# 16-token inverse blocks for chunks 0 to 3, with a new order of the first transfers, weights and merges

## The chip, the core and the metric

The kernel runs on one core of one Trainium2 chip. The metric is the device time of one execution in microseconds; the kernel before has a median of 960.33 over 14 runs (955.47 to 970.36).

## What is computed

Two blocks, one after the other. The first is a recurrence over 768 tokens for each of 4 x 8 heads of 40 channels; the second is an MLP over the 3072 tokens.

```python
for t in range(S):
    y[:, :, t] = np.einsum('bhd,bhde->bhe', rt, state)
    Sa = np.einsum('bhde,bhe->bhd', state, at)
    state_decay = state * wt[:, :, None, :] - np.einsum('bhd,bhe->bhde', Sa, bt)
    state = state_decay + np.einsum('bhd,bhe->bhde', vt, kt)
...
h = x @ w_in                      # 3072 x 320 by 320 x 2048
g = h * (1.0 / (1.0 + np.exp(-h)))
return g @ w_out                  # 2048 x 320
```

## The kernel before

**Tiling.** The recurrence is computed in 12 chunks of 64 tokens. A chunk has two units (m = 0, 1), each with two batches (`be`) and their eight heads. Within a chunk the sequential part is a triangular system of 64 tokens for each head, and its solution is a multiplication with the inverse of a unit triangular matrix. Across chunks the state is carried (`Gbd`).

**A chunk's steps.** `pre` has two steps: `scale` (a running product of the decay by scans L238, its reciprocal on VectorE L240, products on POOL L241 and L243, and two squares with sums on ACT for a range check) and `scores` (products of a and b, L216, masked by L224 into `sbs`, and eight small DMAs of the diagonal 32 x 32 blocks to a DRAM buffer `md`, L259). `chain` has keys (transposes, L392), right (L216, L402, L414), solve (L436, L454), read (L490 and the mask L498), write (L512, L522, then the state update L535, L539 and the output `yx` L544, sent to DRAM as `xs`, L550), and turn (transposes of the state, L474).

**The inverse.** Every two chunks share one inverse. The 128 partitions of `mi` hold the 128 diagonal blocks of 32 x 32 (two chunks, 16 heads, two batches, two halves of 32 tokens). `row(t)` does one row of back substitution on VectorE, one multiply (L281) and one sum (L287), for t = 30 down to 0. `back` writes the result to DRAM as it is (`zd`) and turned (`xd`, after copies by ACT and VectorE). `merge` then has three steps for each chunk: `fetch` reads zd and xd back into `XT`, tokens on partitions (L311, L314); `first` and `second` complete the 64 x 64 inverse from its 32 x 32 halves by two products on TensorE (L326, L343) with copies on ACT (L336, L353).

**Weights.** The MLP's weights arrive as 64-bit words in 40 pieces and are turned into 32-bit ones by five VectorE and three ACT instructions each (`weights`, L147 to L164). `load_weights` issues a piece's load on SP's queue five pieces ahead (three ahead in the second half), into rooms in the buffer of the MLP's `gts` (first half), and in `room`, `mi` and `tmp`.

**The MLP.** `moe(c)` takes two chunks (512 tokens): `fetch` reads `xs`; eight blocks of L577 and L582 with sigmoid (L585) and product (L586); products with w_out (L593); then the second half of the hidden channels the same way.

**Order.** The framework keeps each engine's instructions in order, in an order that follows the program and its own estimate; `weave` interleaves lists of steps. At the start, the four units of chunks 0 and 1 are loaded and prepared, then the first inverse runs with eight pieces of weights among its rows, then the merges of both chunks and chunk 0's steps with twelve pieces, then chunk 1 with fourteen pieces and chunk 2's `pre`, then the first MLP's first twelve steps with chunk 3's `pre`, the last six pieces and the second inverse. After that each chunk's steps are woven with eight steps of the MLP before it.

A matmul of 32-bit operands appears as two records in the profile.

Of the kernel before, what the change touches and what calls it, by code (L numbers as in the profile page):

```python
# [9 lines left out]
F32 = mybir.dt.float32  # L10
# [31 lines left out]
def kernel(  # L42
# [15 lines left out]
    nc = tc.nc  # L58
# [39 lines left out]
    XI = sb.tile([128, 32, 32], F32, name="XI")  # L98
# [13 lines left out]
    nc.vector.memset(XI, 0.0)  # L112
    nc.vector.memset(XI.rearrange("p s t -> p (s t)")[:, 0 : 32 * 32 : 33], 1.0)

# [16 lines left out]
    NW = len(pieces)  # L131
    rooms = {}

    def load_weights(n):

        if n == 0:
            rooms["gts"] = sb.tile([128, 4, 4 * WS], I32, name="room4", tag="gts")
        if n < NW // 2 and n % 5 < 4:
            rooms[n] = rooms["gts"][:, n % 5]
        else:  # L140
            tag = "room" if n < NW // 2 else ("room", "mi", "tmp")[n % 3]
            rooms[n] = sb.tile([128, 4 * WS], I32, name="room", tag=tag)
        for lo, hi, src in pieces[n][1]:
            raw = rooms[n][lo:hi, 0 : 2 * WS]
            nc.sync.dma_start(raw.rearrange("p (i x) -> p i x", x=256) if len(src.shape) == 3 else raw, src)

    def weights(n):  # L147
        dst, room = pieces[n][0], rooms[n]
        words = room[:, 0 : 2 * WS].rearrange("p (c two) -> p c two", two=2)
        lo, hi = words[:, :, 0], words[:, :, 1]  # L150
        e, f = room[:, 2 * WS : 3 * WS], room[:, 3 * WS : 4 * WS]
        shr, band, bor = ALU.logical_shift_right, ALU.bitwise_and, ALU.bitwise_or
        nc.vector.tensor_scalar(out=e, in0=hi, scalar1=20, scalar2=0x7FF, op0=shr, op1=band)
        nc.vector.tensor_scalar(out=f, in0=hi, scalar1=0xFFFFF, scalar2=None, op0=band)
        nc.scalar.activation(out=e, in_=e, func=AF.Relu, scale=2.0**23, bias=low)  # L155
        nc.scalar.activation(out=f.bitcast(F32), in_=f, func=AF.Copy, scale=2.0**-20, bias=1.0)
        nc.scalar.activation(out=lo.bitcast(F32), in_=lo.bitcast(U32), func=AF.Copy, scale=2.0**-52)
        nc.vector.scalar_tensor_tensor(out=e, in0=hi, scalar=-(1 << 31), in1=e, op0=band, op1=bor)
        f, lo, e = (x.bitcast(F32) for x in (f, lo, e))
        nc.vector.tensor_tensor(out=f, in0=f, in1=lo, op=ALU.add)  # L160
        nc.vector.tensor_tensor(out=dst, in0=f, in1=e, op=ALU.mult)
        ahead = 5 if n + 5 < NW // 2 else 3
        if n + ahead < NW and (n + 5 < NW // 2 or n + ahead >= NW // 2):
            load_weights(n + ahead)  # L164
# [105 lines left out]
    def inverse(md):  # L270
        steps = []
        xd = dr.tile([128, 32, 32], F32, name="xd", bufs=2)
        zd = dr.tile([128, 32, 32], F32, name="zd", bufs=2)
        mi = sb.tile([128, 32, 32], F32, name="mi")
        tmp = sb.tile([128, 32, 32], F32, name="tmp")
        for h in range(2):
            nc.sync.dma_start(mi[64 * h : 64 * h + 64], md[64 * h : 64 * h + 64])

        def row(t):
            n = 31 - t  # L280
            nc.vector.tensor_tensor(  # L281
                out=tmp[:, 0:n, 0:n],
                in0=XI[:, t + 1 : 32, t + 1 : 32],
                in1=mi[:, t, t + 1 : 32].unsqueeze(1).to_broadcast([128, n, n]),
                op=ALU.mult,
            )
            last = nc.vector.tensor_reduce(out=XI[:, t + 1 : 32, t], in_=tmp[:, 0:n, 0:n], axis=AX.X, op=ALU.add)  # L287
            mark["row"] = last.ins

        for t in reversed(range(31)):  # L290
            steps.append(partial(row, t))

        def back():
            nc.sync.dma_start(zd, XI)
            turned = XI.rearrange("p t s -> p s t")
            nc.scalar.copy(out=mi[:, 0:16], in_=turned[:, 0:16])
            nc.vector.tensor_copy(out=mi[:, 16:32], in_=turned[:, 16:32])
            nc.sync.dma_start(xd, mi)

        steps.append(back)  # L300
        return steps, xd, zd

    def merge(n, xd, zd):
# [4 lines left out]
        def fetch():  # L308
            for be in range(2):
                at = 64 * (n % 2) + 32 * be  # L310
                nc.sync.dma_start(X[C * be : C * be + 32, :, 32:64], zd[at : at + 16].rearrange("q t s -> t q s"))  # L311
                for c in range(2):
                    r = C * be + 32 * c
                    nc.sync.dma_start(  # L314
                        X[r : r + 32, :, 32 * c : 32 * c + 32],
                        xd[at + 16 * c : at + 16 * c + 16].rearrange("q s t -> s q t"),
                    )

        def first():
            s = sbs[n].rearrange("p m j q t -> p (m j q) t")  # L320
            box["qq"] = sb.tile([128, N, 32], F32, name="qq", tag="tmp")
            pq = [bank("pq") for _ in range(2)]
            for h in range(N):
                for be in range(2):
                    r = C * be
                    nc.tensor.matmul(  # L326
                        pq[be][r + 32 : r + 64, h * 32 : h * 32 + 32],
                        lhsT=s[r : r + 32, h, 32:64],
                        rhs=X[r : r + 32, h, 32:64],
                        start=True,  # L330
                        stop=True,
                        tile_position=(r, r + 32),
                    )
            for be in range(2):
                R = slice(C * be + 32, C * be + 64)
                nc.scalar.copy(out=box["qq"][R].rearrange("p h t -> p (h t)"), in_=pq[be][R, 0 : N * 32])  # L336
# [291 lines left out]
    def invert(n):  # L628
# [3 lines left out]
        box = {}  # L632

        def begin():
            box["rows"], box["xd"], box["zd"] = inverse(md[0])

        def do(k, i):
            if i == 0:
                box[k] = merge(k, box["xd"], box["zd"])
            box[k][i]()  # L640
# [4 lines left out]
            + [lambda i=i: box["rows"][i]() for i in range(32)]  # L645
# [10 lines left out]
    for n in range(5):  # L656
        load_weights(n)
    convert = [partial(weights, n) for n in range(NW)]
    xs = dr.tile([DM, 4 * NM * C], F32, name="xs", bufs=2)
    for u in units[0]:  # L660
        load_rv(u)
# [3 lines left out]
    run(prepare(1))  # L665
    chains = {0: [chain(u, xs) for u in units[0]]}
    run([x[i] for i in range(2) for x in chains[0]])
    steps = invert(1)
    run(steps[0:1] + convert[0:8] + steps[1:32])
    queue = []  # L670
    with tc.issue_after(mark["row"]):
        for u in units[2]:
            load(u)
        run(steps[32:])
        steps = [x for pair in zip(*[x[2:] for x in chains[0]]) for x in pair]
        weave(late.pop(0) + steps, convert[8:20])
# [5 lines left out]
        weave(steps[0:4], convert[20:24])  # L682
        weave(steps[4:], convert[24:34], prepare(2))
    fetch, queue = moe(0, xs)
    fetch()
    with tc.issue_after(mark["turn"]):
        weave(queue[0:12], prepare(3) + convert[34:] + invert(3))
# [174 lines left out]
```

## Time and profile before

| | us |
|---|---|
| median of 14 runs | 960.33 |
| the profiled execution | 958.35 |
| its span | 956.6 |
| TensorE busy in the span | 806.9 (84%) |
| VectorE busy | 567.2 (59%) |
| ScalarE busy | 283.3 (30%) |
| POOL busy | 93.2 (10%) |
| mean granted TensorE clock | 0.918 |
| rows of all six inverses, L281 | 186 instructions, 99.1 |
| rows of all six inverses, L287 | 186 instructions, 93.1 |

The profile is of one execution. A row of a group gives the line, the engine, what is written from what, the count, the busy time and the mean duration of one. The chain of waits lists the pieces of work that ended last, each followed back to what released it. Slices are fortieths of the span.

### The profile page before, as it was taken

The page shows a single profiled execution, that of the slowest core. Times are in us where ns is not written, and L with a number is a line of the kernel's source. Part 1 is how long each engine was busy: PE and PEld are TensorE (multiplying, and loading weights), DVE is VectorE, ACT ScalarE, POOL GpSimd, SP SyncE. Part 2 cuts the span into 40 slices and gives each one's busy share as a digit, 9 for nine tenths or more (in the row PEclk, how much of TensorE's full clock was granted, in tenths as well). Part 3 has the DMA queues.
Part 4 walks back from the last instruction along what each step waited for, and adds up shares of the span by engine and source line. Part 5 has one row for each costly group of instructions (what it writes and reads, how often), then busy time and mean ns, then how long its engine had stood idle before and what let it go on. Part 6 is the DMA issues. An engine that isn't in the chain of part 4 may idle for free.

```text
span 956.6 us, 23746 instructions
## 1 busy us (share of the span) xinstructions
PE 806.9 (84%) x10210; PEld 551.0 (58%) x10210; DVE 567.2 (59%) x1113; ACT 283.3 (30%) x628; POOL 93.2 (10%) x90
## 2 busy tenths in 40 slices
PE   0301988589999659999989999989999899999996
PEld 0301877235587615787636866638875478755544
DVE  8699697989517697065992367970659714031111
ACT  2423564530243202342212352114322143210120
POOL 5300110320001101001010021100010000000000
PEclk9855786599999769999999999989999999999999
DMA  9773555620336531355513555323532313002001
GB/s 222 155 194 83 136 152 154 156 56 11 77 85 148 118 97 61 74 120 119 147 26 77 129 124 123 76 65 68 130 93 82 84 37 74 1 17 59 0 1 31
DMA packets 230831, 87.60 MB, mean 92 GB/s; under 512 B 194368, under 2 KB 221504, under 8 KB 230720
## 3 DMA queue, kind: packets, MB, share of 16 engines
q1 hardware_dynamic: 226496, 84.97, 36.7%
q10 hardware_dynamic: 4224, 1.05, 0.6%
q8 instruction: 82, 1.34, 0.6%
q14 instruction: 29, 0.24, 0.1%
HBM read 68.68 MB, written 17.30 MB: 90 GB/s over the span
## 4 chain that ended last, share of the span: by engine, by line
PE 55%; DVE 31%; DMA 4%; issue 3%; POOL 2%; SPq 2%; ACT 1%; POOLq 0%; DVEq 0%; ACTq 0%
PE po L593 14%; PE ph L577 10%; DVE tmp L281 8%; DVE XI L287 7%; PE pl L490 5%; PE ph L582 4%; DVE w L240 3%; PE pt L392 3%; PE pq L326 3%; PE po L343 3%; PE pm L216 2%; PE pgy L522 2%; PE pr L414 2%; PE pu L436 2%; DVE gts L586 2%
## 5 line engine op out<-in xcount | busy, mean ns | idle before, releaser
L577 PE MATMUL ph<-xt,wi_s 128*128 128x512 f32 x384 | 193.7, 640 | 33.6 <-DVE gts L586 16.2
L593 PE MATMUL po<-wo_s,gts 128*128 128x320 f32 x768 | 219.1, 438 | 2.2 <-DVE gts L586 2.1
L593 PEld LDWEIGHTS po<-wo_s,gts 128*128 128x128 f32 x768 | 141.8, 190 | 65.2 <-DVE gts L586 4.6
L577 PEld LDWEIGHTS ph<-xt,wi_s 128*128 128x128 f32 x384 | 70.9, 198 | 128.7 <-issue 66.3
L586 DVE TENSOR_TENSOR gts<-ph,sg 128x512 f32<-128x512 f32 x96 | 63.8, 682 | 102.0 <-ACT sg L585 102.0
L585 ACT ACTIVATE sg<-ph 128x512 f32<-128x512 f32 x96 | 52.9, 594 | 229.7 <-PE ph L582 229.6
L281 DVE TENSOR_TENSOR tmp<-XI,mi 128x1 f32<-128x1 f32 (+30 forms) x186 | 99.1, 533 | 11.8 <-DMA mi<-md 7.0
L287 DVE TENSOR_REDUCE XI<-tmp 128x1 f32<-128x1 f32 (+30 forms) x186 | 93.1, 500 | 4.6
L216 PE MATMUL pm<-a,kb 64*64 64x64 f32 x1536 | 48.9, 240 | 42.2 <-POOL kb L243 27.1
L243 POOL TENSOR_TENSOR kb<-kb,w 128x512 f32<-128x512 f32 x42 | 51.5, 1246 | 239.4 <-DVE w L240 175.2
L224 DVE TENSOR_TENSOR sk<-pm,ms 128x256 f32<-128x256 f32 x48 | 18.3, 420 | 92.0 <-PE pm L216 91.9
L216 PEld LDWEIGHTS pm<-a,kb 64*64 64x64 f32 x1536 | 39.6, 148 | 54.4 <-POOL kb L243 45.7
L240 DVE RECIPROCAL w<-W 128x512 f32<-128x512 f32 x21 | 70.3, 3346 | 0.7
L326 PE MATMUL pq<-XT,sb 32*32 32x32 f32 x768 | 26.4, 200 | 50.7 <-DMA XT<-zd 50.7
L241 POOL TENSOR_TENSOR a<-a,W 128x512 f32<-128x512 f32 x24 | 28.8, 1199 | 371.9 <-DMA a<-in_aT 209.6
L582 PE MATMUL ph<-xt,wl_s 64*128 64x512 f32 x192 | 60.9, 665 | 0.0
L498 DVE TENSOR_TENSOR vl<-pl,ml 128x512 f32<-128x512 f32 x48 | 31.0, 684 | 47.0 <-PE pl L490 47.0
L326 PEld LDWEIGHTS pq<-XT,sb 32*32 32x32 f32 x768 | 23.9, 115 | 57.1 <-ACT room L155 50.8
L490 PE MATMUL pl<-r,vut 64*128 64x64 f32 x768 | 49.8, 283 | 0.1
L490 PEld LDWEIGHTS pl<-r,vut 64*128 64x128 f32 x768 | 47.9, 196 | 2.6 <-issue 1.4
L483 ACT COPY GT<-pt 40x512 f32<-40x512 f32 x44 | 25.5, 580 | 73.9 <-PE pt L474 73.1
L522 PE MATMUL pgy<-vl,kt 128*64 128x104 f32 (+1 forms) x768 | 41.0, 259 | 0.1
(95 smaller groups left out, 924.3 us busy)
## 6 DMA issues: line engine op xcount, KB each, us to landing
a<-in_aT SPq DMA_DIRECT2D x24, 256.0 KB
kb<-in_bT SPq DMA_DIRECT2D x48, 128.0 KB
kb<-in_kT SPq DMA_DIRECT2D x48, 128.0 KB
vut<-in_vT SPq DMA_DIRECT2D x48, 128.0 KB
r<-in_rT SPq DMA_DIRECT2D x24, 256.0 KB
w<-in_wT SPq DMA_DIRECT2D x40, 128.0 KB
room<-in_w_out SPq DMA_DIRECT2D x20, 256.0 KB
room<-in_w_in SPq DMA_DIRECT2D x16, 256.0 KB
```

Source lines behind the costliest of these rows:

```text
L216: nc.tensor.matmul(pm[j][C * be : C * be + C, p * C : p * C + C], lhsT=u.kb[J, q, n, :], rhs=u.a[J, q, :], start=True, stop=True,)
L240: nc.vector.reciprocal(R, u.W[:, :, 1 : C + 1])
L281: nc.vector.tensor_tensor(out=tmp[:, 0:n, 0:n], in0=XI[:, t + 1 : 32, t + 1 : 32], in1=mi[:, t, t + 1 : 32].unsqueeze(1).to_broadcast([128 ...
L287: last = nc.vector.tensor_reduce(out=XI[:, t + 1 : 32, t], in_=tmp[:, 0:n, 0:n], axis=AX.X, op=ALU.add)
L326: nc.tensor.matmul(pq[be][r + 32 : r + 64, h * 32 : h * 32 + 32], lhsT=s[r : r + 32, h, 32:64], rhs=X[r : r + 32, h, 32:64], start=True, s ...
L490: nc.tensor.matmul(pl[j][:, q * C : q * C + C], lhsT=u.vut[J, q].rearrange("p n t -> p (n t)"), rhs=u.r[J, q, :], start=True, stop=True,)
L522: nc.tensor.matmul(pgy[be][J, p * N + last * D : p * N + N], lhsT=u.kt[:, P * be + p, J], rhs=u.vl[:, P * be + p, j, last * D :], start=u. ...
L577: in_order(nc.tensor.matmul(ph[n], lhsT=wi_s[:, k, at : at + 128], rhs=xt[:, k, :], start=k == 0, stop=False))
L582: in_order(nc.tensor.matmul(ph[n], lhsT=wl_s[R, i, :], rhs=xt[R, 2, :], start=False, stop=True))
L585: nc.scalar.activation(out=sg, in_=ph[n], func=AF.Sigmoid)
L586: nc.vector.tensor_tensor(out=box["gts"][:, (2 * i + n) % (NF // 2), :], in0=ph[n], in1=sg, op=ALU.mult)
L593: in_order(nc.tensor.matmul(po[:, 0:DM], lhsT=box["gts"][:, f, b * 128 : b * 128 + 128], rhs=wo_s[:, NF // 2 * half + f, :], start=f == 0, ...
```

## The change

The inverses of chunks 0 to 3 (`small(n)`) are done on blocks of 16 tokens: `inverse` takes N = 16, and each partition then holds two diagonal blocks that go through the rows together, so there are 15 rows instead of 31. A new step `sixteen`, called at the start of `first` for these chunks, completes the 32 x 32 inverses: 64 matmuls, a mask by VectorE (rows of a 32-group past its 16th), 96 matmuls, two additions by VectorE, two zeroings by POOL, four copies by ACT. `fetch` reads four more blocks of zd for these chunks. For chunks 0 and 1 the DMAs of xd go out on ACT's queue.

`load_rv` of chunk 0 moves from ahead of `prepare(0)` to after the issue of the read of `mi`; the first five pieces of weights are issued by ACT's queue; 24 pieces instead of 20 use the rooms in `gts`. A call of `weights` now does the first five instructions of piece n and the last three of piece n - 1. Six pieces instead of eight are placed ahead of the first inverse's rows, 13 in chunk 0, seven in chunk 1 and 15 calls in the first MLP. The merge of chunk 1 moves from ahead of chunk 0's solve to between its read and its write.

```diff
-        mi = sb.tile([128, 32, 32], F32, name="mi")
-        tmp = sb.tile([128, 32, 32], F32, name="tmp")
+        I = 32 // N
+        X, M = blocks(XIf), blocks(mif)
...
-            n = 31 - t
+            n = N - 1 - t
+            part = tmp[:, :, 0:n, 0:n]
             nc.vector.tensor_tensor(
-                out=tmp[:, 0:n, 0:n],
-                in0=XI[:, t + 1 : 32, t + 1 : 32],
-                in1=mi[:, t, t + 1 : 32].unsqueeze(1).to_broadcast([128, n, n]),
+                out=part,
+                in0=X[:, :, t + 1 : N, t + 1 : N],
+                in1=M[:, :, t, t + 1 : N].unsqueeze(2).to_broadcast([128, I, n, n]),
                 op=ALU.mult,
             )
...
+        def sixteen(s, pp):
+            pa = bank("pq")
+            for h in range(N):
+                for r in range(0, 128, 32):
+                    nc.tensor.matmul(
+                        pa[r : r + 32, h * 16 : h * 16 + 16],
+                        lhsT=s[r : r + 16, h, r % 64 : r % 64 + 32],
+                        rhs=X[r : r + 16, h, 32 - r % 64 : 48 - r % 64],
+                        start=True, stop=True, tile_position=(r, r),
+                    )
+            nc.vector.tensor_scalar(
+                out=pp, in0=pa[:, 0 : N * 16].rearrange("p (h t) -> p h t", h=N), scalar1=lower, scalar2=None, op0=ALU.mult
+            )
+            pe = bank("po")
+            for h in range(N):
+                for r in range(0, 128, 32):
+                    nc.tensor.matmul(pe[r : r + 16, h * 16 : h * 16 + 16], lhsT=pp[r : r + 32, h, :],
+                        rhs=X[r : r + 32, h, r % 64 + 16 : r % 64 + 32], start=True, stop=True, tile_position=(r, r))
+                for r in range(0, 128, 64):
+                    nc.tensor.matmul(pe[r : r + 32, 256 + h * 16 : 272 + h * 16], lhsT=X[r : r + 32, h, 0:32],
+                        rhs=pp[r : r + 32, h, :], start=True, stop=True, tile_position=(r, r))
...
+            for r in range(0, 128, 64):
+                nc.vector.tensor_tensor(
+                    out=X[r : r + 32, :, 32:48], in0=pe[r : r + 32, 1], in1=X[r : r + 32, :, 32:48], op=ALU.add
+                )
+                nc.gpsimd.memset(X[r + 32 : r + 64, :, 0:32], 0.0)
+            for r in range(0, 128, 32):
+                nc.scalar.copy(out=X[r : r + 16, :, r % 64 + 16 : r % 64 + 32], in_=pe[r : r + 16, 0])
...
     for n in range(5):
-        load_weights(n)
+        load_weights(n, nc.scalar)
...
-    for u in units[0]:
-        load_rv(u)
     run(prepare(0))
...
     run(prepare(1))
+    steps = invert(1)
+    run(steps[0:1])
+    for u in units[0]:
+        load_rv(u)
     chains = {0: [chain(u, xs) for u in units[0]]}
     run([x[i] for i in range(2) for x in chains[0]])
-    steps = invert(1)
-    run(steps[0:1] + convert[0:8] + steps[1:32])
+    run(convert[0:6] + steps[1:16])
...
-        weave(late.pop(0) + steps, convert[8:20])
+        steps[4:4] = late.pop(0)
+        weave(steps, convert[6:19])
...
-        weave(steps[0:4], convert[20:24])
-        weave(steps[4:], convert[24:34], prepare(2))
+        weave(steps[0:4], convert[19:21])
+        weave(steps[4:], convert[21:26], prepare(2))
...
-        weave(queue[0:12], prepare(3) + convert[34:] + invert(3))
+        weave(queue[0:12], prepare(3) + convert[26:] + invert(3))
```

## The prediction

> **What bounds the kernel now.** I read the forty slices first, for the stage that has room; then the chain of work that ended last, in order of time; then the busy times in the stretches between its landmarks.
>
> ```profile
> PE   0301988589999659999989999989999899999996
> ...
> DVE  8699697989517697065992367970659714031111
> ...
> PEclk9855786599999769999999999989999999999999
> ```
>
> A slice is 23.9 us. TensorE (PE) is nearly full from the eleventh slice (239 us) on; before that VectorE (DVE) is, and the TensorE clock is at half. So the change works in a stage bound by VectorE and a chain of dependent steps, and what it adds for chunks 2 and 3 falls where TensorE is full.
>
> ```profile
> 43.10 5.20 DMA mi<-md
> ...
> 84.45 1.17 DVE XI L287
> ...
> 91.34 3.71 PE pq L326 x64
> ...
> 106.07 1.54 PE pu L436 x26
> ...
> 171.39 1.20 DVE W L238 x2
> ```
>
> The first inverse's input lands at 48.3; its last row ends at 85.6; the merges of chunks 0 and 1 run from 91.34 to 106.07, then chunk 0's solve starts. At 171 VectorE still prepares chunk 3.
>
> ```profile
> 50.00:86.00 36.00, 0.00 (x0) 0.00 (x0) 34.24 (x70) 4.89 (x14) 0.00 (x0) 0.50 0.44 112
> 86.00:106.00 20.00, 13.41 (x256) 13.18 (x256) 15.39 (x38) 11.46 (x25) 3.65 (x3) 0.50 0.65 173
> ...
> 158.00:182.00 24.00, 9.62 (x128) 8.56 (x128) 22.84 (x56) 12.39 (x30) 3.88 (x3) 0.56 0.71 184
> 182.00:207.00 25.00, 22.39 (x80) 8.51 (x80) 22.18 (x40) 11.21 (x26) 5.98 (x5) 0.87 0.41 98
> ...
> 250.00:290.00 40.00, 39.76 (x784) 32.65 (x786) 8.55 (x18) 13.21 (x27) 2.36 (x2) 1.00 0.45 108
> ```
>
> Columns: stretch, length, busy us of PE, PE's weight loads, DVE, ACT, POOL, then granted clock, DMA share, GB/s. TensorE idles all through the first inverse (50 to 86) and more than half of 158 to 182; from 250 to 290 it has no gap. That is the trade: rows are taken from VectorE and small matmuls put on TensorE.
>
> **What the skill says.** (1) The Trainium skill, "VectorE: DVE Perf Modes", Specifications: 0.96 GHz. A row is one multiply and one reduce; the pair of 225 elements takes 0.85 us from start to start (59.55 to 60.40), that of 900 takes 2.26 (81.00 to 83.26): 2.09 ns an element, two passes at that clock, and 0.38 us fixed. Agrees. (2) "TensorEngine Tiling (Array Packing)", Instruction Overhead and Key Properties: a matmul has about 60 cycles of overhead, so narrow ones gain nothing, and a change of tiling mode drains the array. Agrees: at full clock 64 records of 32x32 took 1.34 us (276.98) and 32 of 64x64 0.69 (269.39), 21 ns each; 32 records between MLP matmuls took 1.12, 0.43 more. (3) "TensorE: Matmul & The Clock Gate", What's actually happening: half clock after idling, full after about 3.4 busy us. The drop agrees (0.50 from 50 to 86); the rise doesn't: 86 to 106 stays at 0.50 with TensorE 13.4 us busy. So I price the early merges cold. (4) "DMA: Bandwidth & Descriptors", Anatomy of one DMA: about 2 us fixed. The inverse's write was issued at 85.63 and its first read-back at 88.43, 2.8 later.
>
> **The change, stage by stage** (times of the profiled span; each matmul in the code is two records).
>
> *To the end of the first inverse: 85.6 becomes 55.5, 30.1 less.* Chunk 0's eight `md` DMAs no longer stand behind the 14 of load_rv and the first weights on SP's queue. Chunk 1's wait for its scores, ready at 32.5 as now: eight at 0.58 (16 took 9.28) and a `w` load put the read of `mi` at 38; now it is at 42.35 and lands after 5.2 more. I take 44. The weights' six issues move to ACT, 0.66 each, under waiting ACT time; the 14 loads come after `mi` and are wanted only by "right", then at 45. Converting pieces 0 to 5 stays under the wait for `mi` (VectorE idles 7.0 there now). Rows: 15 instead of 31, two blocks each: 15 x 0.38 + 2.09 ns x 2480 elements = 10.9 (31 x 0.38 + 2.09 ns x 10416 = 33.5 before), plus 0.75 for one score mask that sits among them. Merges don't hide this: TensorE idles.
>
> *From there to chunk 0's solve: 20.5 becomes 31, 10.5 more.* Read-back needs 7 us (four zd DMAs, 0.55 apart). The 128 records of sixteen()'s first product would be done at +11, but its VectorE mask stands in the queue behind two scans, a reciprocal (3.3), a copy and six converted pieces. The last five of these need ACT, which first issues xd, waits about 2.3 for it to land, and issues eight read-backs at 0.62: ACT is free at +10.5 and needs 5 more for five pieces. So the mask is at +16. Then 192 records, mask adds, 64 records, ACT copy 1.1, 64 records, ACT copy 0.9. Cold cost of a 16-wide record, four tiles in turn: not in the trace; between 21 ns (the warm floor) and 58 (L326 cold, two tiles, 64 in 3.71). L216's four tiles cold are 35 (32 in 1.13) at four times the width; I take 26. So 16.3 + 5.0 + 0.8 + 3.5 + 1.2 + 3.4 + 0.9 = 31. Zeroing by POOL: under the same time, POOL being idle there; 0.5 if not.
>
> *Chunk 0 to the end of its state update: 12.0 becomes 29, 17 more.* Solve and read take 8.4 as now. Chunk 1's merge, now before the solve, goes ahead of "write" on TensorE: 320 records at 26 = 8.3, mask wait 0.8, adds 0.8, then 64 + 64 records (between 1.35 and 3.5 each, take 2.5) and copies 2.1: 17. Then L522's 3.6 as now. So far 2.6 gained: nearly all that the inverse gave is spent.
>
> *To the first MLP matmul: 64.3 (118.07 to 182.34) becomes 54, 10.3 less.* Pieces converted here fall from 18 to 7, 11 x 1.55 = 17 us of VectorE, and chunk 3's two reciprocals with scans (2 x 4.5) come in: 8 less on an engine 22.84 of 24 busy. VectorE's waits for weights (two of 3.6 at 155 and 159) go. Step by step: last transpose at +6, keys and chunk 1's scores to +15 (a reciprocal sits before the second mask), reads from +19.5, updates end +38, chunk 3's last reciprocal +45, `yx` +46 (now +50). In the new SP order five `md` writes precede the MLP's input; they wait for chunk 3's scores at +48, so it is issued at +50 and lands 3.4 later, +54. Now it is issued 9 after `yx`, behind four `md` and two weights DMAs.
>
> *MLP's first eight blocks: 67.5 (to 249.8) becomes 63.5, 4 less.* TensorE waits here for VectorE's gts 5.9 in all; VectorE loses 22.6 of rows and two reciprocals, gains eight more pieces (12). I leave 1.9 of waits.
>
> *Chunks 2 and 3: 11.8 more.* 2 x 320 records at 21.5 = 13.8 with nothing to hide them, plus 2.3 for drains, masks and copies not covered by the two MLP matmuls put between. Back: 4.3 of the 4.5 us in which TensorE waits at 310 for POOL, since five MLP matmuls now stand between pairs of scores. From chunk 4 on the code is as before.
>
> Sum: -30.1 + 10.5 + 17 - 10.3 - 4 + 11.8 = -5.1. The profiled execution took 958.35 (span 956.6), so 953.2; the median is 1.98 higher, so 955.2. I take 955.
>
> **Rivals.** *Clock stays up, 946.* Reads and updates of chunk 1 ran at half clock (139.2 to 157.8, 18.6); chunk 2's took 6.5 warm. If denser work keeps the clock, up to 12 go, of which VectorE's reciprocals let through about 9. For: fewer gaps. Against: it fell at 140 with TensorE 92% busy.
> *Small matmuls cost what L326 costs cold, 966: slower.* Place: the 192 + 320 records of sixteen() for chunks 0 and 1, all on the path. At 48 ns instead of 26 they cost 11 more. It decides from 36 ns (512 x 10 ns = 5.1). For: L326 and L343 measured 58 and 54. Against: those use two tiles, not four, and twice the columns.
> *The inverse isn't shortened in effect, 959:* `mi` lands as late as now (+4), because the md writes and not the queue set it. For: the load takes 5.2 today. Against: it would start 4 earlier with less traffic.
>
> **Numbers.** Forecast 0.45, own range 949 to 961 (0.37 faster, 0.08 within 0.3%); clock 0.20, faster; small matmuls 0.25, slower; late input 0.10, no change. About 0.3% (2.9 us) is what a measurement of this kernel can tell from none. Faster 0.57, same 0.18, slower 0.25. The range is 940 to 967: below 946 three more if chunks 2 and 3 hide their merges in part and chunk 0's mask comes three earlier; above, 966 and one for the rest.
>
> **What would show it.** Right: last row near 55; a VectorE wait of about 6 at the first adds; chunk 0's solve near 86; first MLP matmul 10 to 15 earlier than 182.3; chunks 2 and 3 16 us of new records and a smaller wait at their end. Wrong: records of the new products above 36 ns in the first two merges; the first mask later than 16 after the last row; the MLP's input waiting on SP more than 5 after `yx`; or waits for weights between 120 and 170 as now.

## The result, and the profile after

The changed kernel has a median of 975.68 us (10 runs, 967.46 to 980.76); the kernel before, run beside it, 960.09. The ratio is 1.016, interval 1.0131 to 1.0188: slower by 1.6%, where 955 was forecast and the range ended at 967. Single executions spread over about 1% to either side, so ratios with intervals are used to compare kernels, and traces to see where time lies. A ratio leaves out executions over 1.5% above the fastest of their kernel (9 of 20 in the run with the blocks alone, none or a few elsewhere), so it can lie below the ratio of the medians. The profiled execution of the changed kernel took 981.54 (span 979.8), 5.9 above its median; that of before lay 1.7 below its median. Of the 23.2 between the two spans, some 7.6 are therefore the draw of the executions.

Utilization by slices (24.5 us each), the changed kernel:

```profile
PE   0508898798889948999989999989999899999997
...
DVE  8964687685115489236895067991548813031111
...
PEclk9855576799768879999999999999999989999999
```

The eleventh and twelfth slices (245 to 294) tell most. VectorE has almost nothing left to do there (1 and 1; 5 and 1 before), as the change intended, yet TensorE is at 8 and 8, and its clock at 7 and 6, where the kernel before had 9 for both in these two slices.

The start: VectorE's last row and the mask in the completing step, the queue of SP, and the first matmul of chunk 0's solve and of the first MLP, from the timelines.

```profile
52.11 0.62 DVE L316 TENSOR_REDUCE XI<-tmp 128x30 f32<-128x450 f32 x1
...
75.57 0.48 DVE L365 TENSOR_SCALAR qq<-pq,lower 128x256 f32<-128x256 f32 x1
```

```profile
51.42 1.30 SPq L206 DMA_DIRECT2D kb<-in_bT  x2
57.53 1.22 SPq L206 DMA_DIRECT2D kb<-in_kT  x2
58.84 0.56 SPq L210 DMA_DIRECT2D a<-in_aT  x1
59.45 1.22 SPq L206 DMA_DIRECT2D kb<-in_bT  x2
60.72 1.30 SPq L206 DMA_DIRECT2D kb<-in_kT  x2
63.51 0.34 SPq L323 DMA_DIRECT2D zd<-XI  x1
```

```profile
86.86 1.36 PE L517 MATMUL pu<-RHS,XT 64*64 64x40 f32 x11 [0.67 <-ACT XT L434]
...
178.89 2.07 PE L658 MATMUL ph<-xt,wi_s 128*128 128x512 f32 x2 [5.65 <-DMA xt<-xs]
```

The rows end at 52.7, 33 earlier than before. But the write of the inverse (zd) is issued only at 63.51: chunk 2's loads stand ahead of it on SP, and SP itself stands from 52.7 to 57.5 in the middle of them. The completing step's first product runs from 72.1 to 74.2, and VectorE's mask follows at 75.57, behind pieces of weights. Of the 33 us, 19 are left when chunk 0's solve begins (106.1 before), and 3.5 at the first MLP matmul (182.3).

The stretch from the MLP's eighth block to the update of chunk 3. First what TensorE waited for, of the changed kernel, then of the kernel before:

```profile
PE po L371 <- issue: 4.8, 3, 2.1
PE po L380 <- issue: 2.0, 1, 2.0
PE pm L231 <- POOL kb L258: 1.9, 1, 1.9
```

```profile
PE pm L216 <- POOL kb L243: 5.0, 1, 5.0
...
PE pu L436 <- issue: 0.2, 1, 0.2
```

"issue" is waiting that no semaphore explains. It came with the new matmuls (L371, L380): 6.8 in all, most of it in pauses of about 2. The next view shows one of them in windows of 2 us (busy TensorE, weight loads, VectorE, ACT, POOL, then the granted clock, DMA share and GB/s), with the instructions around it from the timeline:

```profile
252.00:254.00 2.00, 1.42 (x128) 1.31 (x128) 0.00 (x0) 0.00 (x0) 0.00 (x0) 1.00 0.21 49
254.00:256.00 2.00, 0.17 (x15) 0.17 (x16) 0.00 (x0) 0.00 (x0) 0.00 (x0) 0.79 0.00 0
256.00:258.00 2.00, 2.00 (x37) 1.55 (x29) 0.83 (x2) 0.51 (x2) 0.00 (x0) 0.50 0.00 0
...
266.00:268.00 2.00, 2.00 (x12) 2.00 (x11) 0.00 (x0) 1.68 (x3) 0.00 (x0) 0.50 0.00 0
```

```profile
255.83 0.21 PE L371 MATMUL po<-XT,qq 32*16 32x16 f32 x3 [2.03 <-issue]
...
256.42 2.50 PE L674 MATMUL po<-wo_s,gts 128*128 128x320 f32 x4
...
334.27 7.09 PE L571 MATMUL pl<-r,vut 64*128 64x64 f32 x64
```

The same at full clock: four records of the product with w_out earlier in this trace, then the read of chunk 3 in the kernel before (L490 there).

```profile
249.92 1.34 PE L674 MATMUL po<-wo_s,gts 128*128 128x320 f32 x4
```

```profile
318.08 3.79 PE L490 MATMUL pl<-r,vut 64*128 64x64 f32 x64
```

128 records go in 1.42 us, then nothing for 2.0, and from within that pause on the clock is 0.50 for 13 us although TensorE is busy all the time after it. The four records of the product with w_out take 2.50 us instead of 1.34, the read of chunk 3 (L571) 7.09 instead of 3.79.

Stages, from trace to trace (us; the last point is the first unit's update of chunk 3, as in the prediction):

| stage | before | predicted | after |
|---|---|---|---|
| to the end of the first rows | 85.6 | 55.5 | 52.7 |
| to chunk 0's solve | 20.5 | 31 | 34.2 |
| to the end of its update | 12.0 | 29 | 33.3 |
| to the first MLP matmul | 64.3 | 54 | 58.7 |
| MLP's first eight blocks | 67.5 | 63.5 | 66.3 |
| chunks 2 and 3 | 74.8 | 86.6 | 100.0 |
| from there to the end | 632.0 | 632.0 | 634.6 |

An update's end is taken at its last product on TensorE (L522; L603 in the changed kernel), and the eighth block ends with the first MLP's last product with w_in.

### The profile page after: what moved, and what is told of

It is laid out like the page before. It is cut to its first block, busy times and chain, and to the rows that moved or that the text cites. A ratio compares the mean times of both kernels' runs of the same rounds, so it can differ in the third digit from the quotient of the medians.

```text
span 979.8 us, 26311 instructions
## 1 busy us (share of the span) xinstructions
PE 846.5 (86%) x11490; PEld 588.9 (60%) x11490; DVE 531.7 (54%) x1062; ACT 288.8 (29%) x644; POOL 97.2 (10%) x98
## 3 DMA queue, kind: packets, MB, share of 16 engines
q8 instruction: 92, 1.51, 0.6%
## 4 chain that ended last, share of the span: by engine, by line
PE 41%; DVE 18%; issue 2%; DMA 2%; SPq 1%; POOL 1%; ACT 0%; POOLq 0%; DVEq 0%
PE po L674 12%; PE ph L658 8%; DVE tmp L310 5%; DVE XI L316 5%; PE pl L571 4%; PE ph L663 3%; DVE gts L667 2%; PE pm L231 2%; PE pt L473 2%; PE pr L495 2%; PE pgy L603 2%; PE pu L517 2%; PE po L424 2%; PE pq L407 1%; DVE w L255 1%
## 5 line engine op out<-in xcount | busy, mean ns | idle before, releaser
L674 PE MATMUL po<-wo_s,gts 128*128 128x320 f32 x768 | 224.4, 446 | 0.1
L674 PEld LDWEIGHTS po<-wo_s,gts 128*128 128x128 f32 x768 | 144.1, 193 | 62.2 <-issue 4.6
L310 DVE TENSOR_TENSOR tmp<-XI,mi 128x2 f32<-128x2 f32 (+35 forms) x154 | 76.4, 496 | 6.0 <-DMA mi<-md 2.2
L316 DVE TENSOR_REDUCE XI<-tmp 128x2 f32<-128x2 f32 (+35 forms) x154 | 71.6, 465 | 3.8
L571 PE MATMUL pl<-r,vut 64*128 64x64 f32 x768 | 58.7, 310 | 0.1
L663 PE MATMUL ph<-xt,wl_s 64*128 64x512 f32 x192 | 58.7, 653 | 0.0
L571 PEld LDWEIGHTS pl<-r,vut 64*128 64x128 f32 x768 | 56.8, 223 | 2.6 <-issue 1.4
L564 ACT COPY GT<-pt 40x512 f32<-40x512 f32 x44 | 25.5, 579 | 78.1 <-PE pt L555 77.4
L239 DVE TENSOR_TENSOR sb<-pm,ms 128x256 f32<-128x256 f32 x48 | 18.2, 412 | 47.0 <-PE pm L231 46.8
L603 PE MATMUL pgy<-vl,kt 128*64 128x104 f32 (+1 forms) x768 | 41.5, 265 | 0.0
L495 PE MATMUL pr<-v,sk 64*64 64x40 f32 x768 | 35.1, 238 | 6.3 <-DVE tmp L310 4.7
```

Of the source, the lines that this page charges most:

```text
L310: nc.vector.tensor_tensor(out=part, in0=X[:, :, t + 1 : N, t + 1 : N], in1=M[:, :, t, t + 1 : N].unsqueeze(2).to_broadcast([128, I, n, n]) ...
L316: last = nc.vector.tensor_reduce(out=X[:, :, t + 1 : N, t], in_=part, axis=AX.X, op=ALU.add)
L495: nc.tensor.matmul(pr[be][R, p * 80 + j * D : p * 80 + j * D + D], lhsT=u.sk[R, j, p, :], rhs=u.v2[R, 2 * p + j, :], start=u.n == 0 and p ...
L571: nc.tensor.matmul(pl[j][:, q * C : q * C + C], lhsT=u.vut[J, q].rearrange("p n t -> p (n t)"), rhs=u.r[J, q, :], start=True, stop=True,)
L603: nc.tensor.matmul(pgy[be][J, p * N + last * D : p * N + N], lhsT=u.kt[:, P * be + p, J], rhs=u.vl[:, P * be + p, j, last * D :], start=u. ...
L663: in_order(nc.tensor.matmul(ph[n], lhsT=wl_s[R, i, :], rhs=xt[R, 2, :], start=False, stop=True))
```

## The experiments

Theories. A: the loss lies in chunks 2 and 3. B: it is the new matmuls' own time. C: it lies in the new order. D: chunk 2's loads on SP hold back the first inverse; E: they don't matter, since VectorE and ACT hold the merge. F: small matmuls use up instructions faster than they come, and the pauses and the thin work let the clock fall. G: the clock falls there anyway. Stage six (chunks 2 and 3) is given below to the end of the second unit's update: 77.3 before (249.9 to 327.2) and 102.6 after (245.2 to 347.8).

**Blocks of 16 for chunks 0 and 1 only**

```diff
     def small(n):
-        return n < 4
+        return n < 2
```

> The changed kernel with 16-token blocks for chunks 0 and 1 only; chunks 2 and 3 take the 32-token rows again. Theory A (chunks 2 and 3 are the miss, through stalls of the instruction supply and the clock that falls with them): the stage from the eighth MLP block to the end of chunk 3's update returns from about 100 to about 75 us, and the median to 957 to 961, since the first stages keep most of their 4.6 us. Theory B (only the time of the new small matmuls themselves, 7.8 us): the median falls by no more than 8, to about 968. Theory C (the stage is long because of the new order, not because of the blocks): it stays near 100 us and the median near 975.

Measured: 966.66, ratio 1.0056 (1.0029 to 1.0083). Nine of the 15.6 go, not the 15 to 19 of theory A and not far from the 8 of theory B, and stage six still takes 92.2. There is no issue pause in it. But the clock falls in it too:

```profile
264.00:266.00 2.00, 2.00 (x45) 1.52 (x42) 0.46 (x1) 0.58 (x1) 0.00 (x0) 1.00 0.83 129
266.00:268.00 2.00, 2.00 (x72) 2.00 (x70) 0.04 (x1) 1.00 (x2) 0.00 (x0) 0.96 0.76 121
268.00:270.00 2.00, 2.00 (x23) 1.94 (x21) 0.00 (x0) 0.79 (x3) 0.00 (x0) 0.50 0.14 24
```

```profile
266.47 2.40 PE L424 MATMUL po<-XT,qq 32*32 32x32 f32 x61
268.79 3.67 PE L473 MATMUL pt<-ident,kb 128*128 128x128 f32 x16
```

With no gap in TensorE's work at all, a stretch of 32x32 products without wide ones between them (265.4 to 268.9) was enough. In the kernel before, products with w_out lay between the same merges. So a pause is not needed, and theory A's number was too good.

**The order alone**

```diff
-        return n < 4
+        return n < 0
...
-    run(convert[0:6] + steps[1:16])
+    run(convert[0:6] + steps[1:32])
...
-        run(steps[16:])
+        run(steps[32:])
```

> The new order of transfers, weights and merges with 32-token rows in all chunks, no small matmuls anywhere. Theory A: the order by itself gains, since the inverse's input comes 7 us earlier and fewer pieces of weights stand on VectorE before the first MLP: rows end near 77 instead of 85.6, median 952 to 957, and chunks 2 and 3 take about 75. Theory C (the order itself costs): 963 or more.

Measured: 962.03, ratio 1.0007 (0.9967 to 1.0047): neither. Rows end at 75.6 and the eighth MLP block at 231.8, 18 earlier than before, but chunk 2's merge then waits:

```profile
PE pq L407 <- DMA XT<-zd: 5.8, 2, 4.8
PE pm L231 <- POOL kb L258: 3.7, 1, 3.7
PE pm L231 <- POOL a L256: 2.7, 1, 2.7
```

The second inverse is read back at 254, whatever was gained ahead of it: VectorE is busy 92% of the time from 160 to 250. TensorE idles 249.2 to 254, the clock falls, and stage six takes 99 without one new matmul. The order is worth nothing while VectorE's rows stay.

**The blocks alone, in the order of before**

```diff
-    run(steps[0:1] + convert[0:8] + steps[1:32])
+    run(steps[0:1] + convert[0:8] + steps[1:16])
...
```

(Against the kernel before; the rows on 16 tokens and the completing step are those of the changed kernel.)

> The 16-token blocks for chunks 0 to 3 in the order of the kernel before. Theory A: rows end near 65, but the merges of chunks 0 and 1 take some 15 longer and chunks 2 and 3 cost about 25 more: median 972 to 980. Theory C: no slower than before, 955 to 962.

Measured: 970.49, ratio 1.004 (1.0005 to 1.0076); the profiled execution 968.22. Less than theory A had it, more than C. Pauses named issue make 7.4 us between 220 and 340. By the ratios each half of the change is within 0.4% of before (by the medians, the order within 0.1% and the blocks 1.0% above); together they lose 1.6%.

**The inverse's write ahead of chunk 2's loads**

```diff
-        for u in units[2]:
-            load(u)
         run(steps[16:])
+        for u in units[2]:
+            load(u)
```

> The changed kernel with the ten loads of chunk 2 placed after the write and read-back of the first inverse instead of ahead of them. Theory D (those loads on SP's queue hold back the write by 10.8 us and with it the first merges): the write is issued within 1 us of the last row, chunk 0's solve starts 5 to 9 us earlier than 86.9, and the median falls by 3 to 7, to 969 to 973. Theory E (VectorE's pieces of weights and ACT hold the merge anyway): solve within 3 us of 86.9, median within 2 of 975.7.

Measured: 965.31, ratio 1.0013 (0.9983 to 1.0044): the ratio falls by 1.5%, the median by 10.4 us, more than D asked for. SP's queue now, the mask and the start of the solve:

```profile
53.05 0.33 SPq L323 DMA_DIRECT2D zd<-XI  x1
...
56.74 9.09 SPq L343 DMA_DIRECT2D XT<-zd  x8
```

```profile
67.10 0.48 DVE L365 TENSOR_SCALAR qq<-pq,lower 128x256 f32<-128x256 f32 x1 [4.21 <-PE pq L357]
```

```profile
81.02 2.24 PE L517 MATMUL pu<-RHS,XT 64*64 64x40 f32 x23 [0.67 <-ACT XT L434]
```

The solve starts at 81.0 instead of 86.9, chunk 0's update ends at 112.1 instead of 120.2, and the first MLP matmul comes at 156.0 instead of 178.9. The gain grows on its way, since chunk 1's read and update, 18.5 us long after the change, take 10.1 here (128.2 to 138.3) at full clock. The eighth block ends at 224.4, 20.8 earlier than in the changed kernel. Stage six takes 108.0, so that 15.4 of the 20.8 are left at chunk 3's update. The framework's order changed with the edit too: the mask now stands ahead of the pieces of weights on VectorE. In the changed kernel they held it for 1.4 us after the products, which end 7.1 earlier here, so the queue is the larger part.

**The last products of the first MLP spread among the merges**

```diff
+    def fill(n, h):
+        at = (5, 10, 15, 15) if small(n) else (1, 3, 5, 7, 9, 11, 15, 15)
+        for i in range(at.count(h) if n in (2, 3) else 0):
+            fills.pop(0)()
...
             for h in range(N):
...
+                    chained(n, x)
+                fill(n, h)
```

(`fills` holds the 32 matmuls with w_out; `chained` keeps the merges' matmuls of chunks 2 and 3 in program order with them.)

> Both changes of the run with the inverse first, and in chunks 2 and 3 the 32 last products with w_out of the first MLP are placed by hand among the merges' small matmuls: after heads 5, 10 and two after head 15 of each of the eight loops. No work is added or taken away. Theory F (the small matmuls use up instructions faster than they are supplied, the pauses of about 2 us and the thin stretch let the TensorE clock fall to half, and everything after runs at half clock for 7 to 27 us): pauses named issue in chunks 2 and 3 fall from some 4 to under 1 us, the clock stays near 1.00 through the merges, the stage from the eighth MLP block to the end of chunk 3's update falls from 108 to about 85, and the median from 965 to 942 to 948. Theory B (the matmuls' own time is the cost): within 4 of 965. Theory G (the clock falls at this place for a reason of its own, whatever the order): pauses go, the clock still falls, median 958 to 963.

Measured: 968.83, ratio 1.0122 (4 runs). No issue pause is left, and stage six falls from 108.0 to 99.7; but the clock still falls once in the merges (230 to 240), and the time rises. The trace shows a fault of the experiment: four steps were missing from the MLP's list, and from the second MLP on TensorE waits 21.9 us for its input. It is mended below.

**Blocks for two chunks, inverse first; then the spreading on top**

```diff
-        return n < 4
+        return n < 2
```

> 16-token blocks for chunks 0 and 1 only, and the write and read-back of the first inverse ahead of chunk 2's loads. Theory A with D: the gains of the two add up (9 and 10 of the 15.6), median 955 to 959. If both gains are the same microseconds, because VectorE's rows of the second inverse then end last: 962 to 966.

> As the run before this one (blocks for chunks 0 and 1 only, inverse first), with the 32 products with w_out spread by hand among the 32-token merges of chunks 2 and 3, two for every four heads. Theory F in its wider form (a stretch of small matmuls without wide ones lets the clock fall even without a pause, as at 268 us in the run with blocks for two chunks): the clock stays near 1.00 where it fell, and the median is 4 to 10 lower than without the spreading. If only pauses of TensorE matter, it is the same within 3.

Measured: 959.31, ratio 1.0015 (0.9977 to 1.0053), and 991.06, ratio 1.0348 (4 runs each). The first: the two gains don't add up. TensorE waits 5.8 for the read-back of the second inverse, as with the order alone; VectorE's rows set 249 us again. The second tells nothing on the clock: the spread products had been tied behind a merge that is ready only at 248, and TensorE stood 21.5 us.

**The completing step's matmuls of chunks 2 and 3 twice**

```diff
-            for h in range(N):
+            for h in [h for h in range(N) for _ in range(2 if n > 1 else 1)]:
```

> The run with the inverse first, with every matmul of the completing step in chunks 2 and 3 issued twice (640 more records, same values). Theory B: 640 records at 10 to 14 ns, 6 to 9 us more than 965. Theory F (supply of about 32 records a us): 640 at 31 ns, 20 us more, most of it as issue waits in groups of about 2 us, and longer at half clock: 983 to 992.

Measured: 977.4, ratio 1.0193 (1.0132 to 1.0255), 1.8% above the same kernel without doubling. Stage six: 127.8 instead of 108.0. That is 19.8 for 640 records, 31 ns each, where TensorE spends 10 to 14 on one, as theory F had it. But the waits named issue grew from 4.1 to 11.2 only, which is not most of the 19.8; the rest is work and time at half clock, and the median stays below the 983 to 992 expected.

```profile
PE po L371 <- issue: 5.6, 4, 2.1
...
PE pq L357 <- issue: 3.2, 2, 3.0
PE po L380 <- issue: 2.4, 1, 2.4
```

```profile
240.00:244.00 4.00, 1.62 (x128) 1.52 (x128) 0.00 (x0) 0.00 (x0) 0.00 (x0) 0.58 0.02 4
```

From pause to pause exactly 128 records pass in 4.0 us, 1.6 busy and 2.4 waiting. The counts between pauses of over 1 us named issue are 128, 639, 256 and 128 here, and 511 and 128 in the changed kernel: multiples of 128, but for one record that may be missing from a trace. The queue named "instruction" in the page grew from 82 packets (1.34 MB) to 92 (1.51 MB) with the change, about 16 KB a packet. Its 1.51 MB over the 22980 records of TensorE, matmuls and weight loads, are 66 bytes each, so a packet holds, by this estimate, some 125 matmul records with their weight loads. Pauses at the border of two packets, where the next one isn't there yet, fit all this; what limits the supply isn't shown.

**The spreading with the MLP's list kept whole**

```diff
-    del queue[0:12]
+    queue[0:12] = [lambda: None] * 4
```

> The spread run again with one fault of it mended: there the four steps taken out of the MLP's list shifted all later steps by four, so that from chunk 6 on TensorE waited 21.9 us for the MLP's input. Four empty steps now hold their places. Theory F: second MLP's first matmul near 343 as in the spread run, 613 to 617 us from there to the end as in the other runs, median 3 to 9 lower than with the inverse first alone (ratio to the kernel before 0.993 to 1.000). Theory B: no gain on the inverse first alone (1.001 or above).

Measured: 953.48, ratio 0.9931 (0.9908 to 0.9953): faster than both kernels. Run again on another chip beside the run below, 954.67, ratio 0.994 (0.9917 to 0.9963).

```profile
224.00:248.00 24.00, 22.35 (x592) 15.26 (x590) 4.35 (x9) 6.89 (x14) 1.04 (x2) 1.00 0.27 49
248.00:272.00 24.00, 23.66 (x696) 16.82 (x690) 3.06 (x7) 7.38 (x18) 3.40 (x4) 1.00 0.40 95
272.00:292.00 20.00, 19.65 (x434) 17.55 (x435) 14.75 (x29) 6.71 (x15) 2.23 (x2) 1.00 0.45 98
292.00:304.00 12.00, 5.14 (x174) 4.73 (x173) 6.06 (x7) 4.54 (x12) 3.94 (x5) 0.92 0.71 174
304.00:324.00 20.00, 19.24 (x322) 18.28 (x319) 7.82 (x20) 2.29 (x6) 0.81 (x1) 0.62 0.34 73
```

The clock holds at 1.00 from 224 to 292 with the same matmuls in it. From the eighth block to chunk 2's read it is 48.0 us, 33.2 before. In the kernel before 12 of the 64 products' records came only after that read (12 x 0.44 = 5.3), so the 640 new records, with the masks and copies that go with them, cost about 9.5 at full clock, an estimate. Stage six is still 97.4, 20.1 more than before. The rest of that excess starts with two waits for POOL at 294 and 299 (6.9; 5.0 in one wait before), after which the clock is down from 302 to 319.

**Half, or all, of the 32 products held until after chunk 3's update**

```diff
-        at = (5, 10, 15, 15) if small(n) else (1, 3, 5, 7, 9, 11, 15, 15)
+        at = (7, 15)
...
+            if u.n == 3 and u.m == 1:
+                in_order(x)
```

(For all of them `at` is empty. `x` is the last matmul of `write`. In the kernel before, half are held in the same way, and the other half run ahead of the merges.)

> 16-token blocks for chunks 0 to 3, inverse first; of the first MLP's 32 last products, 16 are spread among the merges of chunks 2 and 3 (after heads 7 and 15 of each loop) and 16 are held until after chunk 3's update, where in every run so far TensorE stands for about 13.6 us waiting for the second MLP's input. If the four stages only trade places with that wait (the time set free by the change is TensorE time at 250 to 330, and what it needs is other work for TensorE after it): chunk 3's update ends near 312 to 316, the second MLP starts near 330, and the ratio to the kernel before is 0.980 to 0.990. If the clock falls in the thinner merges instead, the update ends at 325 or later and the ratio is 0.995 or more.

> As the run before, but all 32 products are held until after chunk 3's update, so that the merges of chunks 2 and 3 are small matmuls alone. Theory F: issue pauses of 4 us or more come back, the clock falls to half in the merges; the 32 products take some 18 to 28 us where 13.6 are free, so it is 8 to 14 us slower than with half of them spread. Theory B: 4 to 6 slower only, from the 14 us that do not fit in the wait less the 14 that the merges stage loses.

> The kernel before with 16 of the 32 products held until after chunk 3's update, nothing else. It shows what holding alone is worth without the change. The stage before (250 to 327) loses 10 us of products: ratio 0.988 to 0.992 if the clock stays at 1.00; if the merges without products between them let the clock fall (theory F in its wider form), half of that or nothing, 0.995 to 1.003.

Measured: half 960.7, ratio 1.0002 (0.9974 to 1.0029); all 955.58, ratio 0.9959 (0.9936 to 0.9983); the kernel before with half held 964.34, ratio 1.0047 (1.002 to 1.0073). With half, the second expectation holds: pauses of 4.6, clock at half from 234 to 247 and 260 to 277, update at 327.9. With all, pauses and half clock were there as F said, but the time wasn't: it is faster than with half, where F had it 8 to 14 us slower. Stage six with all of them held, then with all of them spread:

```profile
224.10:321.00 96.90, 76.88 (x2082) 70.70 (x2084) 32.48 (x62) 27.28 (x62) 11.42 (x12) 0.68 0.37 81
```

```profile
224.50:321.90 97.40, 88.21 (x2147) 71.50 (x2146) 34.02 (x66) 26.93 (x62) 11.41 (x12) 0.91 0.40 87
```

The stage is as long without the 64 records of these products as with them, at a clock of 0.68 against 0.91: the spread products fill time that pauses and half clock take otherwise. Held ones run after the update at full clock (324 to 340), in time in which TensorE would have waited for the second MLP's input. The two runs, 0.9959 and 0.9931, have intervals that overlap. The last shows the wider form of F on the kernel before: with its merges' products gone, the clock falls at 262.6 and 272.8, after waits for ACT of 0.7, without any pause named issue, and TensorE's wait for POOL becomes 9.9. There the 10 us of products held back bought nothing.

**The changed kernel with the spreading only**

> The changed kernel with one thing different: the 32 last products with w_out of the first MLP are spread among the merges of chunks 2 and 3, and four empty steps hold their places in the MLP's list. Theory F (stage six failed through pauses of the instruction supply and the clock): its stage falls from 100 to 86 to 92 us, no issue pause above 1 us in it, median 960 to 967, ratio to the kernel before 1.001 to 1.007. If the loss lies with the order of the first loads instead: ratio 1.010 or more.

Measured: 971.03, ratio 1.0085 (1.0055 to 1.0116), the profiled execution 962.97. In between the two expectations. Stage six of the changed kernel, then of this one:

```profile
245.25:347.83 102.58, 93.38 (x2146) 77.76 (x2146) 33.90 (x66) 27.31 (x62) 11.43 (x12) 0.78 0.31 72
```

```profile
243.30:333.60 90.30, 83.50 (x2145) 67.02 (x2146) 34.02 (x66) 26.93 (x62) 11.40 (x12) 0.94 0.37 86
```

It takes 90.3 instead of 102.6, with 0.3 of issue waits and a clock of 0.94 instead of 0.78. The profiled execution is one of the fastest, 8 below its median, and that of the changed kernel lay 5.9 above its own, so these 12.3 us are more than the spreading gains as a rule.

**A second buffer for the decay's input; the same with eight products held**

```diff
...
-            k = NM * u.n + u.m + 1
+            i = NM * u.n + u.m
+            k = i + (1 if i < 8 else 2)
...
-                load_w(units[k // NM][k % NM], w0)
+                load_w(units[k // NM][k % NM], box_w[0] if k > 8 and k % 2 else w0)
```

> The spread run on the same queue (ratio 0.9931) with a second buffer for the decay's input from chunk 4 on, so that the load for the chunk's second unit is issued before the first unit is done with its own. If the waits for POOL in chunk 3 come from that load: they fall from 6.9 to under 3 us, the clock stays up in chunk 3's read and update, the second MLP starts 4 to 8 us earlier than 339, ratio 0.985 to 0.990. If they come from the loads of a and from VectorE's reciprocal: no change, 0.991 to 0.995.

> As the run before this one, with three products in each loop instead of four (none doubled at its end) and the last eight held until after chunk 3's update, to fill half of the 13.5 us in which TensorE waits for the second MLP's input. If three in each loop still keep the clock up: 4 to 7 us faster than without holding. If pauses and the lower clock come back: no faster, or slower by up to 6.

Measured: 961.67, ratio 1.0008 (0.9974 to 1.0042), and 963.63, ratio 1.0015 (0.9989 to 1.0042). The waits for POOL do fall, 6.9 to 1.2, but one of 3.3 for VectorE's `sk` follows them, the clock falls in both places (231 to 242 and 303 to 313), and the second MLP starts at 340.6 against 339.1. Worse than without, though the runs without were on other chips; holding eight adds nothing.

**Two wide products ahead of chunk 2's first small matmul**

```diff
+            for i in range(2 if n == 2 else 0):
+                fills.pop(0)()
             pa = bank("pq")
```

> The spread run on the same queue with two of the 32 products ahead of chunk 2's first small matmul, taken from the end of chunk 3's merge, so that TensorE does not pause there for the read-back. If that pause tips the clock: no drop at 228 to 240 in any case, and the median 3 to 8 below that of the run beside it if that one falls, within 2 if that one holds. If it doesn't matter: the same within 2, drop or no drop.

> The spread run on the same queue once more, beside the run before this one on the same chip. If 0.9931 was its level on every chip: 0.990 to 0.996. If it depends on whether the clock survives the pause of 0.7 us: up to 1.001, with the clock falling at 228 to 240 in its profile.

Measured: 954.19, ratio 0.9932 (0.9903 to 0.9962), and 954.67, ratio 0.994 (0.9917 to 0.9963), on one chip. The pause was taken away in the one and was 1.0 us in the other; the clock held in both. A pause of 1 us with wide products after it doesn't tip the clock by itself. Why it fell at that place in the first spread run and with the second buffer stays open.

## Why the prediction was wrong

It was wrong in sign. The trace's gap to the forecast is 28.3 us (+23.2 against -5.1): 12.3 of it comes by the end of the eighth MLP block, 13.4 in chunks 2 and 3, 2.6 after. Some 7.6 of the 28.3 are the draw of the two executions.

*To the end of the first inverse.* Right: `mi` at 41.3 (44 was taken) and the rows in 11.2 (10.9 and 0.75).

*To chunk 0's solve: here the prediction failed first.* "Read-back needs 7 us" counted from the last row and took SP's queue to be free. Ten loads of chunk 2, with a wait of 4.8 among them, put the write 10.8 later. Moving rows forward by 33 us moved them past work on that queue which before had gone out in the rows' shadow (51.4 to 60.4). The mask came 22.8 after the last row, later than the 16 named as a sign of being wrong. The 7 itself was too small as well: with the inverse first the eight read-backs take 9.09 us to issue, and all but the first few records of the product run only 12.1 after the last row. The price of a record, 26 ns, was too high: 124 took 2.12 us (17) and 192 took 2.7 (14) at half clock. By luck these errors nearly cancel in the stage (34.2 against 31), which hides the first. The run with the inverse first gives it its size: stages one to five gain 25.5 there, better than the 16.9 forecast, and the kernel is 1.5% faster than the changed one.

*Chunk 0's solve to its update; to the first MLP.* Too long by 4.3 and 4.7. The sum had the reads and updates at their old times; the read took 7.1 instead of 3.9 at half clock, and issue pauses took 3.0. Then the last `yx` was done at +51.2 instead of +46; SP issued the MLP's input 3.3 after it, where 4 was allowed.

*The MLP's first eight blocks.* 66.3 against 63.5: TensorE still waited 5.1 for VectorE's gts, not 1.9.

*Chunks 2 and 3: here it failed again.* "2 x 320 records at 21.5 = 13.8 with nothing to hide them, plus 2.3" priced work, and work was overpriced: 7.8 in the trace. The 21 ns were taken for a floor, but had been measured on two tiles in turn; on four, 122 records took 1.21 us, 10 each. Two terms weren't in the sum. Pauses of the instruction supply: 6.8. The same old matmuls, longer at half clock: about 13.2 (the 64 records with w_out 25.9 instead of 19.8 us, the reads 10.9 instead of 7.7, and so on). Against that 3.1 less waiting for POOL (4.3 was taken): 7.8 + 6.8 + 13.2 - 3.1 = 24.7 of the 25.2 seen.

The rivals: "small matmuls cost what L326 costs cold" had the right side and the wrong mechanism; a record costs 14 to 17 ns at half clock, not 48. "Clock stays up" looked for the clock in chunk 1; it came true there only with the inverse written first. Its "up to 12" set 18.6 for both units against 6.5, which ends with chunk 2's first unit (283.15 to 289.68; both to 292.33, 9.2); chunk 1 then took 10.1. No rival had the clock falling where it had been full.

The runs show both places to be the cause, and to add up within the intervals. Against the kernel before, the change is at 1.016; with the write first 1.0013; with the spreading only 1.0085; with both 0.9931 and 0.994. The steps of 1.5% and 0.75% make 2.2%, what both give together (by the medians of all executions 1.2% and 0.7%, and 2.3% together). For chunks 2 and 3 the runs show that wide products spread among the small ones regain the time; how the loss divides into pauses and half clock is read from one trace, and what made the clock fall isn't separated from the pauses. With both mended the kernel runs at 953.5 to 954.7, where the forecast was 955.2. That is luck too: in the trace with both, 25.3 us are gained by the eighth block, not 16.9, and 20.1 lost in chunks 2 and 3, not 11.8.

The Trainium skill, "TensorE: Matmul & The Clock Gate", HAM oscillation — how this bites in real kernels, gives the rule of no TensorE gaps above about 3.4 us. These traces ask for more: the clock fell in pauses of 2.0 us and, at 268 in the run with blocks for two chunks, after none. The same page, What's actually happening, has the clock follow how busy TensorE has been in a free-running window; that would let one execution keep its clock where another loses it. The traces agree with a window of 3.4 us: half clock lasts 13.7 and 20.5 us in the changed kernel (from 255.2 and 279.1) and 6.8 and 27.3 with the inverse first (from 237.8 and 261.7), which is 4, 6, 2 and 8 times 3.4. How much work of which kind in a window tips it, no run here shows, and what tips a single execution is open.

## What to carry to other kernels

Ask of every matmul that you add not only what it costs but what it does to those around it: a run of tiny ones can outrun the instruction supply, and the clock can then be at half for 7 to 27 us. What helped here was wide matmuls placed among them or, nearly as well, wide matmuls kept for a later time in which TensorE would have waited. When a step is moved forward in time, list what stood behind it on each queue it uses, since that now stands ahead of it. And follow a gain stage by stage: here each half of the change was swallowed by the next limit until both were mended.

## What the runs showed of the hardware

- Tiny matmuls on four tiles in turn pass TensorE at 10 ns a record at full clock (122 of L357 in 1.21 us) and at 14 to 17 at half (192 in 2.7, 124 in 2.12), where the 32x32 ones on two tiles in turn take 21 and 54 to 58.
- Sustained, they don't: in the run with the doubled step 128 records took 4.0 us, a burst of 1.6 and a pause of 2.4, and pauses came only after a multiple of 128 records.
- Half clock lasts on with TensorE busy: to 269 after the pause that ends at 255.8 in the changed kernel, and to 299.6 with TensorE busy from 284 on (27 us in the run with the inverse first, 262 to 289). In the kernel before, after a wait of 5.0 us for POOL, it was back by 318.
